# Attention and maxout feed-forward: weights cast to bf16 on their way in, by transfers that GpSimd queues

## The chip, the cores and the metric

The kernel runs on one core of a Trainium2 chip. A core has a matrix engine (TensorE, PE in the profile, with PEld for its weight loads), three engines for elementwise work (VectorE or DVE, ScalarE or ACT, GpSimd or POOL), and SyncE (SP), which here only queues transfers between the chip's memory and the core's on-chip memory. Sixteen DMA engines carry the transfers out. The metric is the device time of one execution in microseconds (us).

## The reference

The inputs are q, k and v of shape 4 x 8 x 768 x 64 (batch, heads, sequence, head size) and four weight matrices, all fp32. Attention is local, with a few global keys and a distance bias; its output feeds a maxout feed-forward:

```python
scores = scale * np.matmul(q, k.transpose(0, 1, 3, 2))
keep = (pos[None, :] < 8) | ((rel >= 0) & (rel < 96))   # rel = query position - key position
scores = np.where(keep, scores - slope[h] * dist, -1e9)
a = softmax(scores)
x = (a @ v) as (3072, 512)
h = np.maximum(np.maximum(x @ w1, x @ w2), x @ w3)      # w1, w2, w3: 512 x 768
out = h @ w_out                                         # w_out: 768 x 512
```

## The kernel before

The 3072 tokens are 24 tiles of 128, six for each batch. Attention of a tile needs only its own keys, those of the tile before it and the eight global keys, so it is a small job. The feed-forward works on chunks of 4, 2, 2, 4, 4, 4 and 4 tiles, and most of TensorE's work is there.

Everything is cut into units, and one long string, `SCHEDULE`, lists them in the order in which each engine, and each transfer queue, gets its instructions. Each engine then runs its own instructions strictly in this order and waits where an operand or a buffer is not ready. A unit is a letter with numbers. Where there is a last number that says who copies or casts, 0 is ScalarE, 1 VectorE and 2 GpSimd, 3 and 4 are mixtures or a transpose by DMA. The units that matter here:

- `l`, `v`, `L`: loads of q and k (512 KB each for the parts of the first twelve tiles, 256 KB for q or k of a later tile) and of v (256 KB a tile), queued by SP (lines 158, 174 and 167). `c` and `C` cast them to bf16 (lines 183, 189 and 198), `x` and `X` transpose q and k (tile `tpp`, line 239). `l0.0` and `l0.1` stand ahead of the string. Part 0 of the `l` and `x` units holds tiles 0 and 1, part 1 tiles 2 and 3, part 2 tiles 4 and 5, part 3 tiles 6 to 9. `l2.1` is k of tiles 4 and 5, `l3.0` a half of the heads of q of tiles 6 to 9.
- `G`, `V`: overwrite the first eight rows of a tile's k or v with the global ones (lines 214 to 216, and 221).
- `S`: scores of a tile for four heads, with the exponential on ScalarE. The mask and bias come either by a matmul against a bias tile ahead of the scores (last number 1, line 275) or by a multiplication on VectorE afterwards (unit `M`, line 307). `K` and `B` build the two kinds of tables.
- `A`: attention times v (lines 322 and 325), then the division by the row sum on VectorE (331 and 332). `T`: transpose of the result into `xT` (line 349).
- `F c.f.j`: chunk c, hidden block f (128 wide), weight matrix j: four matmuls (line 361) and a copy or maximum. `O`: the output product of a tile (line 376), its copy, and the store by SP (line 383). `E`: the last of these.
- `D`: matmuls on zeros at the start (line 436).
- `w g.j`, `o i`: loads of weights, queued by SP, fp32, into staging buffers (`wst`, `wost`, lines 417 and 422). `w0.j` is columns 0 to 255 of matrix j (512 KB), `w1.j` columns 256 to 767 (1 MB), `o` a third of w_out (512 KB).
- `W g.j`, `Q i`: casts of staged weights to bf16 into the tiles `w123` (three tiles, by column block) and `wo` (lines 427 and 430).

So a weight passes through an SP transfer, a staging buffer and a cast. The three `W` casts of columns 0 to 255 read `w0`, the other six read a half each of `w1`. There are three buffers of each size, and `o` shares those of `w0`.

Of the kernel before, what the change touches and what calls it, by code (L numbers as in the profile page):

```python
# [22 lines left out]


SCHEDULE = """
    K0 K1 K2 l1.0 B0.2 B1.1 B2.1 K3 K4 K5 K6 B3.0 B4.1 l1.1 D1.4 B5.0 c0.0.2 B6.0 c0.1.1 D0.4 v0 l2.0
    x0.0.3 K7 x0.1.4 c1.0.1 v1 l2.1 B7.0 S0.0.1 S0.1.1 G0.2 S1.0.0 M0.0 M0.1 c1.1.1 c2.0.2 x1.0.2 x1.1.0
    C0.1.1 A0.0 S1.1.1 G1.1 v2 v3 S2.0.1 S2.1.0 G2.1 T0.1 M1.0 M1.1 c2.1.1 S3.0.1 M2.0 M2.1 C1.1.2
    C2.1.1 M3.0 S3.1.1 M3.1 A1.0 V1.2 x2.0.2 C3.1.2 w0.0 A2.1 x2.1.0 V2.2 A3.0 T1.0 w0.1 G3.2 W0.0.2
    T2.1 T3.1 S4.0.0 S4.1.0 w0.2 F0.0.0 F0.1.0 W0.2.1 G4.2 w1.0 W0.1.2 F0.0.1 F0.1.1 F0.0.2 F0.1.2  # L30
    S5.0.0 S5.1.0 V3.2 M4.0 W1.0.2 F0.2.0 M4.1 M5.0 F0.3.0 v4 w1.1 W2.1.0 W2.0.2 F0.4.0 F0.5.0 W1.1.1
    C4.1.2 w1.2 W1.2.2 M5.1 v5 A4.1 l3.0 l3.2 l3.1 C5.1.0 V4.2 F0.2.1 c3.0.0 F0.3.1 F0.4.1 T4.0 F0.5.1
    A5.1 F0.2.2 c3.2.0 F0.3.2 W2.2.2 F0.4.2 x3.0.2 T5.1 F0.5.2 x3.2.1 F1.0.0 F1.1.0 l3.3 l4.0 F1.0.1
    F1.1.1 c3.1.2 c3.3.2 F1.0.2 x3.1.4 F1.2.0 F1.2.1 x3.3.1 F1.3.0 c4.0.0 o2 F1.1.2 o1 Q1.1 F1.4.0 Q2.2
    S6.0.0 S6.1.0 G6.2 M6.0 o0 F1.5.0 F1.2.2 F1.3.1 S7.0.0 S7.1.0 v6 l4.1 v7 F1.4.1 G7.0 M6.1 v8 F1.3.2
    x4.0.0 L12 v9 M7.0 L13 Q0.2 O0.0.1 S8.0.0 M7.1 c4.1.1 S8.1.0 C6.1.2 F1.5.1 O0.1.0 A6.0 x4.1.2 C7.1.2
    A7.1 V7.1 G8.2 F1.4.2 F1.5.2 S9.0.0 S9.1.0 G9.2 v10 T6.1 M8.0 O0.2.1 T7.1 C8.1.0 v11 S10.0.0 S10.1.0
    G10.0 M8.1 M9.0 M9.1 O0.3.0 A8.0 F2.0.0 V8.2 F2.1.0 F2.0.1 F2.1.1 C9.1.2 C12.0.2 C13.0.2 C10.1.0
    F2.0.2 F2.1.2 A9.1 M10.0 M10.1 V9.1 X12.0 F2.2.0 F2.3.0 S11.0.0 S11.1.0 T8.4 M11.0 X13.4 F2.4.0 L14
    O1.0.1 L15 T9.0 F2.2.1 A10.1 F2.5.0 V10.2 F2.3.1 F2.4.1 S12.0.0 S12.1.0 M11.1 M12.0 F2.2.2 F2.3.2  # L40
    F2.4.2 v12 C11.1.2 A11.0 C14.0.0 X14.4 T10.0 v13 v14 M12.1 v15 F2.5.1 C12.1.2 F2.5.2 O1.1.1 G12.1
    S13.0.0 S13.1.0 G13.1 T11.1 O2.0.0 F3.0.0 M13.0 F3.0.1 M13.1 F3.1.0 F3.2.0 A12.1 C15.0.0 F3.0.2
    S14.0.0 X15.4 S14.1.0 T12.4 C13.1.1 F3.1.1 F3.2.1 v16 L16 L17 G14.0 L18 A13.0 F3.1.2 F3.2.2 F3.3.0
    M14.0 T13.1 F3.3.1 F3.3.2 V13.2 S15.0.0 S15.1.0 G15.0 F3.4.0 C14.1.2 F3.5.0 M14.1 M15.0 M15.1 A14.0
    V14.2 F3.4.1 F3.5.1 T14.4 F3.4.2 C15.1.2 F3.5.2 A15.0 L19 v17 C16.0.2 C17.0.2 X16.0 O2.1.0 X17.4
    T15.1 S16.0.0 v18 v19 S16.1.0 C18.0.2 G16.0 M16.0 O3.0.1 O3.1.1 F4.0.0 V15.2 F4.1.0 F4.2.0 F4.3.0
    C16.1.2 M16.1 A16.1 C19.0.2 X18.3 X19.4 F4.0.1 F4.0.2 S17.0.0 S17.1.0 M17.0 F4.1.1 C17.1.1 F4.1.2
    S18.0.0 S18.1.0 C18.1.1 F4.2.1 F4.3.1 T16.4 M17.1 F4.2.2 F4.3.2 G18.0 S19.0.0 M18.0 M18.1 L20 M19.0
    C19.1.1 L21 S19.1.0 F4.4.0 F4.5.0 G19.2 V16.2 C20.0.0 L22 A17.0 F4.4.1 M19.1 F4.5.1 F4.4.2 F4.5.2
    X20.4 T17.4 A18.1 T18.4 A19.0 T19.4 O3.2.0 O3.3.0 C21.0.1 C22.0.0 O4.0.0 S20.0.0 S20.1.0 M20.0 X21.4  # L50
    v20 G20.0 V19.1 M20.1 O4.1.0 F5.0.0 F5.1.0 F5.2.0 F5.0.1 F5.1.1 S21.0.0 S21.1.0 F5.0.2 F5.3.0 F5.1.2
    C20.1.2 A20.1 G21.1 X22.4 V20.2 F5.4.0 L23 F5.5.0 S22.0.0 S22.1.0 v21 v22 v23 C21.1.2 C22.1.2
    C23.0.0 X23.4 M21.0 M21.1 M22.0 F5.2.1 F5.3.1 F5.4.1 F5.5.1 F5.2.2 C23.1.1 F5.3.2 A21.1 F5.4.2
    F5.5.2 G22.2 S23.0.0 T20.4 S23.1.0 T21.4 O4.2.0 M22.1 M23.0 M23.1 V21.2 A22.0 O4.3.0 V22.2 A23.1
    T22.4 T23.4 O5.0.0 O5.1.0 O5.2.0 O5.3.0 F6.0.0 F6.1.0 F6.2.0 F6.0.1 F6.1.1 F6.0.2 F6.2.1 F6.1.2
    F6.3.0 F6.2.2 F6.4.0 F6.5.0 F6.3.1 F6.4.1 F6.3.2 F6.4.2 F6.5.1 F6.5.2 E
"""


# [1 line left out]
def kernel(  # L61
# [293 lines left out]
    def u_F1(c, f, j):  # L355
        W = len(chunks[c]) * 128
        if f == 0 and j == 0:
            ht[c] = ht_pool.tile([128, NF, W], BF16, name="ht", tag="ht")
        ps = psH.tile([128, W], FP32, name="h", tag="h")
        for dm in range(4):  # L360
            nc.tensor.matmul(ps, w123[f // 2][:, dm, j, (f % 2) * 128:(f % 2) * 128 + 128],  # L361
                             xT[c][:, dm], start=(dm == 0), stop=(dm == 3))
# [49 lines left out]
    def load_w(g, j):

        n = 256 * (1 + g)
        st = stage_pool.tile([128, 4, n], FP32, name="wst", tag=f"wst{g}")
# [1 line left out]
        nc.sync.dma_start(out=st, in_=wsrc[j][:, 256 * g:256 * g + n].rearrange("(i p) f -> p i f", p=128))
# [92 lines left out]
```

## Time and profile before

| | |
|---|---|
| median of 17 runs | 181.29 us (180.58 to 183.16) |
| the profiled execution | 181.41 us, of which the span from first to last instruction is 179.6 us |
| HBM read, written | 25.17 MB, 6.29 MB |
| SP queue (q1) | 83424 packets, 35.20 MB |
| first F matmul starts | 23.85 us |
| `w0`, `w1` transfer, issue to landing | 7.0 us (512 KB), 10.7 us (1 MB), medians |
| casts of weights | POOL 1038 ns x6 and 1042 ns x2, DVE 787 ns x2 and 1565 ns x1, ACT 1078 ns x1 |

Times in the views are microseconds from the first instruction; "x" gives the number of instructions. A chain of waits is followed back from the last instruction to whatever released each step. Matmul ends are modelled and matmuls overlap, so PE's busy time says little about how full it is; the list of its waits says more. The DMA share is the mean busy share of sixteen engines and passes 1 where packets overlap.

### The profile page before, as it was taken

How to read it: one execution, taken by the hardware profiler on the slowest of the kernel's cores; microseconds unless marked ns; L12 is line 12 of the kernel's file. 1: busy time of each engine (PE TensorE's matmuls, PEld its weight loads, DVE VectorE, ACT ScalarE, POOL GpSimd, SP SyncE). 2: the span in 40 equal slices, each digit the busy share in tenths (PEclk: the TensorE clock that was granted, in tenths of full speed). 3: DMA queues.
4: the chain of work that ended last, by engine and by line, in shares of the span. 5: the costliest groups of instructions: out<-in, count | busy, mean ns of one | idle time of the engine just before them, and what ended most of it. 6: DMA issues, size and time to landing. Idle time of an engine off the chain costs nothing.

```text
span 179.6 us, 3985 instructions
## 1 busy us (share of the span) xinstructions
PE 169.5 (94%) x1556; PEld 95.7 (53%) x1556; DVE 121.6 (68%) x236; ACT 103.2 (57%) x158; POOL 38.8 (22%) x66
## 2 busy tenths in 40 slices
PE   7587799999999999999999999999999999999991
PEld 2343644558867687755555554454445555444450
DVE  4566548788998988957887648996346994053810
ACT  4999664853787956569162566344965353513031
POOL 6313555424430152010224600100011211000000
PEclk9999999999999999999999999999999999999999
DMA  5999999999999658997499999954999624700014
GB/s 138 290 263 250 337 341 385 318 335 367 258 215 252 157 148 204 202 205 153 99 223 180 237 181 269 227 103 95 210 234 218 118 50 146 262 0 4 0 67 167
DMA packets 83586, 35.51 MB, mean 198 GB/s; under 512 B 66160, under 2 KB 78320, under 8 KB 83568
## 3 DMA queue, kind: packets, MB, share of 16 engines
q1 hardware_dynamic: 83424, 35.20, 84.8%
q8 instruction: 12, 0.20, 0.5%
q10 hardware_dynamic: 144, 0.07, 0.1%
q14 instruction: 6, 0.05, 0.1%
HBM read 25.17 MB, written 6.29 MB: 175 GB/s over the span
## 4 chain that ended last, share of the span: by engine, by line
PE 84%; SPq 5%; DMA 4%; issue 3%; POOL 1%; DVE 1%; ACT 0%; ACTq 0%; POOLq 0%
PE h L361 53%; PE po L376 17%; PE sp L283 6%; SPq L158 3%; DMA rawp<-in_k_dram 3%; PE op L322 3%; PE op L325 3%; SPq L174 2%; PE tpp L239 1%; PE xtp L349 1%; DMA out_dram<-ost 1%; PE tp L261 1%; POOL va L221 0%; DVE xb L332 0%; POOL va L189 0%
## 5 line engine op out<-in xcount | busy, mean ns | idle before, releaser
L361 PE MATMUL h<-xT,w 128*128 128x512 bf16 (+1 forms) x504 | 100.1, 349 | 0.1
L361 PEld LDWEIGHTS <-w 128*128 128x128 bf16 x504 | 47.0, 98 | 40.7 <-issue 0.6
L288 ACT ACTIVATE P<-sp 128x1024 bf16<-128x1024 f32 (+1 forms) x48 | 43.3, 954 | 21.7 <-PE sp L283 21.3
L368 DVE TENSOR_TENSOR h<-h,h 128x512 bf16<-128x512 bf16 (+1 forms) x42 | 25.3, 608 | 19.0 <-PE h L361 18.5
L376 PE MATMUL po<-wo,ht 128*128 128x512 bf16 (+2 forms) x156 | 33.6, 363 | 0.0
L366 ACT CAST h<-h 128x512 bf16<-128x512 f32 (+1 forms) x42 | 21.6, 534 | 19.2 <-PE h L361 18.6
L307 DVE TENSOR_TENSOR P<-P,wmask 128x1024 bf16<-128x1024 bf16 x36 | 25.3, 716 | 7.4 <-ACT P L288 7.3
L370 DVE TENSOR_TENSOR ht<-h,h 128x512 bf16<-128x512 bf16 (+1 forms) x42 | 25.2, 607 | 5.2 <-PE h L361 4.2
L376 PEld LDWEIGHTS <-ht 128*128 128x128 bf16 x156 | 14.1, 98 | 13.8
L382 ACT COPY ost<-po 128x512 f32<-128x512 f32 (+2 forms) x19 | 10.6, 561 | 18.1 <-PE po L376 15.6
L332 DVE TENSOR_TENSOR xb<-op,rz 128x512 bf16<-128x512 f32 x24 | 16.6, 691 | 0.8
L283 PEld LDWEIGHTS <-qkT 64*128 64x128 bf16 x352 | 10.0, 94 | 9.1 <-issue 7.8
L283 PE MATMUL sp<-qkT 64*128 64x128 bf16 x352 | 14.7, 219 | 0.0
L322 PEld LDWEIGHTS <-P 128*128 128x128 bf16 x192 | 12.5, 97 | 3.5 <-DVE P L307 0.5
L221 POOL COPY va<-vaf 8x260 int32<-8x260 int32 x13 | 6.2, 478 | 35.6 <-PE op L325 32.3
L322 PE MATMUL op<-va,P 128*128 128x65 bf16 x160 | 12.6, 193 | 1.1 <-POOL va L189 0.8
L189 POOL CAST va<-rawv 128x512 bf16<-128x512 f32 x12 | 7.6, 633 | 23.1 <-PE h L361 17.4
L325 PEld LDWEIGHTS <-P 128*128 128x128 bf16 x160 | 10.5, 97 | 2.3 <-issue 0.9
L243 ACT COPY qkT<-tpp 128x1024 bf16<-128x1024 bf16 (+1 forms) x9 | 8.2, 920 | 3.5 <-PE tpp L239 3.2
L239 PE MATMUL tpp<-identb,qkp 128*128 128x128 bf16 x96 | 8.2, 234 | 2.0 <-POOL qkp L183 1.6
L325 PE MATMUL op<-va,P 128*128 128x65 bf16 x128 | 9.9, 193 | 0.2 <-POOL va L221 0.2
L331 DVE RECIPROCAL rz<-op 128x8 f32<-128x8 f32 x24 | 4.9, 204 | 7.4 <-PE op L325 5.7
(69 smaller groups left out, 114.2 us busy)
## 6 DMA issues: line engine op xcount, KB each, us to landing
rawv<-in_v_dram SPq DMA_DIRECT2D x24, 256.0 KB, 5.3
out_dram<-ost SPq DMA_DIRECT2D x23, 256.0 KB, 2.3
rawp<-in_q_dram SPq DMA_DIRECT2D x6, 512.0 KB, 7.3
rawp<-in_k_dram SPq DMA_DIRECT2D x6, 512.0 KB, 7.3
wst<-in_moe_w_dram SPq DMA_DIRECT2D x3, 1024.0 KB, 10.7
raw<-in_q_dram SPq DMA_DIRECT2D x12, 256.0 KB, 4.9
raw<-in_k_dram SPq DMA_DIRECT2D x12, 256.0 KB, 4.9
wst<-in_moe_w_dram SPq DMA_DIRECT2D x3, 512.0 KB, 7.0
```

The source lines that it names most:

```text
L283: nc.tensor.matmul(sp[:, hh, j2, ds], qT(T - ds, 1)[hsl, jp], qT(T, 0)[hsl, jp], start=not how, stop=True, skip_group_check=True)
L288: nc.scalar.activation(P[:, :, 0:n], sp.rearrange("p a b d n -> p (a b) d n")[:, :, 0:n], AF.Exp, bias=0.0, scale=scale)
L307: nc.vector.tensor_mul(P, P, wmask[:, g, :, 0:2])
L322: nc.tensor.matmul(o, P[:, i, 0], heads(va[T])[:, h], start=True, stop=(t == 0), skip_group_check=True)
L325: nc.tensor.matmul(o, P[:, i, 1], heads(va[T - 1])[:, h], start=False, stop=True, skip_group_check=True)
L332: nc.vector.tensor_tensor(out=x.rearrange("p (g h) d -> p g h d", g=2), in0=o4[:, :, :, 0:64], in1=rz[:, :, :, None].to_broadcast([128, 2, ...
L361: nc.tensor.matmul(ps, w123[f // 2][:, dm, j, (f % 2) * 128:(f % 2) * 128 + 128], xT[c][:, dm], start=(dm == 0), stop=(dm == 3))
L366: nc.scalar.copy(h01, ps)
L368: nc.vector.tensor_max(h01s[c, f], h01s[c, f], ps)
L370: nc.vector.tensor_max(ht[c][:, f], h01s[c, f], ps)
L376: nc.tensor.matmul(po, ht[c][:, f, tt * 128:(tt + 1) * 128], wo[:, f, cols], start=(f == 0), stop=(f == NF - 1))
L382: copy(ost, po)
```

## The change

SP no longer loads the weights. GpSimd queues them, in one transfer each from fp32 in memory to bf16 in the persistent tile, with the same rows and sizes at the source. The staging pool is gone. The units `W` and `Q` remain in the string but do nothing. `w123` is one tile in place of three; each F matmul waits for the transfer that brought its columns. `SCHEDULE` is a different string from its first line to its last: the order of units, and who copies or casts what, are new, while the units of loads, scores, attention and feed-forward are the same in number. The `D` units no longer occur. Scores with the bias by matmul are now S0.0, S0.1, S1.1, S2.1, S3.0, S3.1, S4.0 and S6.0; before they were S0.0, S0.1, S1.1, S2.0, S3.0 and S3.1.

In the new order SP's first transfers are: q and k of part 0, q and k of part 1, q of part 2, v of tiles 0, 1, 2, 3, k of part 2 (`l2.1`), `l3.0`, `l3.2`, v of tiles 4 and 5. GpSimd's instructions after its set-up are: two q casts, cast of v of tile 0, `w0.0`, cast of v of tile 1, `w0.1`, `w0.2`, `w1.0`, `w1.1`, patch V2.2, `w1.2`, cast of `l3.0`, cast of `l3.1`, the three `o`. VectorE casts `l2.1` ahead of v of tile 3.

The start of the string, up to the first F units:

```diff
-    K0 K1 K2 l1.0 B0.2 B1.1 B2.1 K3 K4 K5 K6 B3.0 B4.1 l1.1 D1.4 B5.0 c0.0.2 B6.0 c0.1.1 D0.4 v0 l2.0
-    x0.0.3 K7 x0.1.4 c1.0.1 v1 l2.1 B7.0 S0.0.1 S0.1.1 G0.2 S1.0.0 M0.0 M0.1 c1.1.1 c2.0.2 x1.0.2 x1.1.0
-    C0.1.1 A0.0 S1.1.1 G1.1 v2 v3 S2.0.1 S2.1.0 G2.1 T0.1 M1.0 M1.1 c2.1.1 S3.0.1 M2.0 M2.1 C1.1.2
-    C2.1.1 M3.0 S3.1.1 M3.1 A1.0 V1.2 x2.0.2 C3.1.2 w0.0 A2.1 x2.1.0 V2.2 A3.0 T1.0 w0.1 G3.2 W0.0.2
-    T2.1 T3.1 S4.0.0 S4.1.0 w0.2 F0.0.0 F0.1.0 W0.2.1 G4.2 w1.0 W0.1.2 F0.0.1 F0.1.1 F0.0.2 F0.1.2
...
+    K0 l1.0 l1.1 K1 l2.0 c0.0.0 B0.2 B1.1 B2.1 B3.1 B4.0 B5.2 K2 x0.0.3 c0.1.0 x0.1.4 K3 K4 S0.0.1 K5
+    B6.1 c1.0.2 v0 x1.0.0 B7.1 S0.1.1 G0.0 c1.1.1 v1 c2.0.2 S1.0.0 x1.1.4 S1.1.1 G1.1 x2.0.3 C0.1.2
+    S2.0.0 w0.0 C1.1.2 v2 S2.1.1 w0.1 K6 M0.0 K7 M0.1 w0.2 M1.0 M1.1 w1.0 A0.0 v3 G2.0 w1.1 M2.0 A1.1
+    V1.1 W0.2.1 C2.1.0 S3.0.1 l2.1 c2.1.1 S3.1.1 C3.1.1 M2.1 A2.0 G3.1 x2.1.2 T0.0 V2.2 w1.2 M3.0 M3.1
+    A3.1 T1.0 S4.0.1 l3.0 l3.2 v4 v5 W0.0.0 W1.0.1 T2.1 T3.1 S4.1.0 c3.0.2 c3.2.1 l3.1 c3.1.2 V3.1
+    W0.1.2 W2.1.1 l3.3 W1.1.1 G4.1 x3.0.2 F0.0.0 F0.1.0 M4.0 M4.1 l4.0 v6 W2.2.2 S5.0.0 S5.1.0 v7 o1
+    x3.2.3 l4.1 F0.0.1 F0.1.1 W1.2.1 o2 o0 S6.0.1 W2.0.1 F0.0.2 F0.1.2 Q0.1 M5.0 M5.1 C4.1.0 A4.1 F0.2.0
...
```

The functions:

```diff
-    stage_pool = ctx.enter_context(tc.tile_pool(name="stage", bufs=3))
...
-    w123 = [persist.tile([128, 4, 3, 256], BF16, name=f"w123_{i}") for i in range(3)]
+    w123 = persist.tile([128, 4, 3, DFF], BF16, name="w123")
...
-            nc.tensor.matmul(ps, w123[f // 2][:, dm, j, (f % 2) * 128:(f % 2) * 128 + 128],
+            nc.tensor.matmul(ps, w123[:, dm, j, f * 128:f * 128 + 128],
                              xT[c][:, dm], start=(dm == 0), stop=(dm == 3))
...
         n = 256 * (1 + g)
-        st = stage_pool.tile([128, 4, n], FP32, name="wst", tag=f"wst{g}")
-        wst[g, j] = st
-        nc.sync.dma_start(out=st, in_=wsrc[j][:, 256 * g:256 * g + n].rearrange("(i p) f -> p i f", p=128))
+        nc.gpsimd.dma_start(out=w123[:, :, j, 256 * g:256 * g + n],
+                            in_=wsrc[j][:, 256 * g:256 * g + n].rearrange("(i p) f -> p i f", p=128))
...
     def load_wo(i):
-        st = stage_pool.tile([128, 2, DM], FP32, name="wost", tag="wst0")
-        wst["o", i] = st
-        nc.sync.dma_start(out=st, in_=moe_w_out[i * 256:(i + 1) * 256, :].rearrange(
-            "(i p) f -> p i f", p=128))
+        nc.gpsimd.dma_start(out=wo[:, 2 * i:2 * i + 2],
+                            in_=moe_w_out[i * 256:(i + 1) * 256, :].rearrange("(i p) f -> p i f", p=128))
...
     def cast_w(g, j, how):
-        src = wst[0, j] if g == 0 else wst[1, j][:, :, 256 * (g - 1):256 * g]
-        copies[how](w123[g][:, :, j], src)
+        pass
...
     def cast_wo(i, how):
-        copies[how](wo[:, 2 * i:2 * i + 2], wst["o", i])
+        pass
```

More of the change, by code (lines that the diff above doesn't have):

```diff
@@ L31 @@
[L31 to L55, printed above, removed]
@@ L56 @@
-    F6.3.0 F6.2.2 F6.4.0 F6.5.0 F6.3.1 F6.4.1 F6.3.2 F6.4.2 F6.5.1 F6.5.2 E
+    K0 l1.0 l1.1 K1 l2.0 c0.0.0 B0.2 B1.1 B2.1 B3.1 B4.0 B5.2 K2 x0.0.3 c0.1.0 x0.1.4 K3 K4 S0.0.1 K5
[3 more added lines that the diff above has]
+    A3.1 T1.0 S4.0.1 l3.0 l3.2 v4 v5 W0.0.0 W1.0.1 T2.1 T3.1 S4.1.0 c3.0.2 c3.2.1 l3.1 c3.1.2 V3.1
@@ new lines @@
+    W0.1.2 W2.1.1 l3.3 W1.1.1 G4.1 x3.0.2 F0.0.0 F0.1.0 M4.0 M4.1 l4.0 v6 W2.2.2 S5.0.0 S5.1.0 v7 o1
+    x3.2.3 l4.1 F0.0.1 F0.1.1 W1.2.1 o2 o0 S6.0.1 W2.0.1 F0.0.2 F0.1.2 Q0.1 M5.0 M5.1 C4.1.0 A4.1 F0.2.0
+    F0.3.0 F0.4.0 F0.5.0 V4.1 C5.1.1 T4.1 A5.0 M6.0 F0.2.1 F0.3.1 F0.4.1 F0.5.1 F0.2.2 F0.3.2 F0.4.2
+    T5.0 x3.1.2 c3.3.1 F0.5.2 x3.3.0 v8 v9 F1.0.0 F1.0.1 F1.0.2 S6.1.0 G6.2 M6.1 S7.0.0 F1.1.0 F1.2.0
+    S7.1.0 F1.1.1 c4.0.2 x4.0.4 C6.1.2 F1.3.0 F1.4.0 C7.1.0 G7.2 M7.0 M7.1 S8.0.0 S8.1.0 F1.2.1 F1.3.1
@@ new lines @@
+    F1.4.1 F1.1.2 F1.2.2 Q2.2 F1.3.2 F1.4.2 G8.2 L12 c4.1.0 C12.0.2 A6.1 F1.5.0 A7.0 x4.1.0 C8.1.0 Q1.0
+    O0.0.0 M8.0 M8.1 T6.1 v10 S9.0.0 V7.1 M9.0 S9.1.0 M9.1 v11 v12 O0.1.0 O0.2.1 A8.0 T7.0 O0.3.0 F2.0.0
+    V8.2 G9.2 S10.0.0 S10.1.0 G10.2 F1.5.1 L13 F2.0.1 L14 T8.0 C9.1.1 C10.1.2 C11.1.0 F1.5.2 F2.0.2
+    M10.0 S11.0.0 M10.1 M11.0 S11.1.0 M11.1 C13.0.2 F2.1.0 X12.1 O1.0.0 A9.1 F2.2.0 F2.3.0 O1.1.1 F2.1.1
+    T9.0 V9.2 A10.0 V10.2 F2.2.1 F2.3.1 F2.4.0 S12.0.0 S12.1.0 X13.4 F2.1.2 F2.5.0 T10.0 L15 A11.0
@@ new lines @@
+    F2.4.1 F2.5.1 F2.2.2 C14.0.2 X14.4 T11.0 G12.1 S13.0.0 S13.1.0 v13 F2.3.2 F2.4.2 F2.5.2 F3.0.0
+    F3.1.0 M12.0 M12.1 F3.0.1 G13.1 F3.0.2 L16 M13.0 v14 L17 M13.1 F3.2.0 S14.0.0 S14.1.0 M14.0 F3.1.1
+    F3.2.1 C12.1.2 A12.0 C13.1.0 L18 C14.1.0 C15.0.2 X15.1 M14.1 F3.3.0 v15 F3.4.0 F3.3.1 A13.0 V13.2
+    T12.4 F3.1.2 C16.0.0 A14.1 G14.1 C17.0.1 F3.5.0 X16.4 X17.4 F3.2.2 F3.4.1 C18.0.1 T13.4 S15.0.0
+    S15.1.0 M15.0 T14.4 F3.5.1 F3.3.2 M15.1 F3.4.2 V14.2 X18.0 L19 L20 v16 v17 O2.0.0 C15.1.2 A15.1
@@ new lines @@
+    O2.1.1 T15.1 F3.5.2 G15.0 S16.0.0 S16.1.0 G16.1 F4.0.0 F4.1.0 S17.0.0 S17.1.0 M16.0 F4.2.0 F4.0.1
+    F4.1.1 S18.0.0 S18.1.0 V15.1 F4.0.2 C19.0.2 M16.1 M17.0 C16.1.2 X19.4 O3.0.0 v18 M17.1 C17.1.0 M18.0
+    C18.1.2 F4.3.0 A16.1 O3.1.1 V16.1 F4.1.2 T16.4 v19 C19.1.2 O3.2.1 G18.0 v20 S19.0.0 S19.1.0 M18.1
+    M19.0 M19.1 O3.3.0 C20.0.0 X20.4 F4.4.0 F4.2.1 A17.1 F4.5.0 T17.4 F4.2.2 A18.1 T18.4 F4.3.1 A19.0
+    F4.4.1 F4.5.1 V19.2 F4.3.2 F4.4.2 G19.0 S20.0.0 S20.1.0 M20.0 T19.4 F4.5.2 L21 C20.1.2 L22 C21.0.3
@@ new lines @@
+    F5.0.0 F5.1.0 G20.1 M20.1 F5.0.1 F5.1.1 F5.0.2 F5.1.2 A20.1 F5.2.0 X21.4 L23 C22.0.3 X22.4 F5.3.0
+    F5.4.0 F5.2.1 F5.3.1 C23.0.1 v21 S21.0.0 M21.0 S21.1.0 G21.2 F5.5.0 V20.1 F5.4.1 v22 M21.1 S22.0.0
+    S22.1.0 G22.0 C21.1.2 C22.1.2 T20.4 F5.2.2 F5.3.2 X23.4 A21.0 M22.0 v23 C23.1.2 F5.5.1 F5.4.2 F5.5.2
+    S23.0.0 S23.1.0 O4.0.0 M22.1 M23.0 M23.1 O4.1.0 T21.4 V21.2 A22.0 V22.2 O4.2.0 T22.4 A23.1 T23.4
+    O4.3.0 O5.0.1 O5.1.0 O5.2.1 F6.0.0 F6.0.1 F6.1.0 F6.0.2 F6.1.1 F6.2.0 F6.3.0 F6.4.0 O5.3.1 F6.2.1
@@ L57 @@
+    F6.3.1 F6.4.1 F6.1.2 F6.5.0 F6.2.2 F6.3.2 F6.4.2 F6.5.1 F6.5.2 E
 """
```

## The prediction

> **What bounds the kernel now.** I read the page's header and chain of waits first, then a table of stages, then PE's waits stage by stage, then the timelines of SP and GpSimd up to 36 us. Header and chain:
>
> ```profile
> span 179.6 us, 3985 instructions
> PE 169.5 (94%) x1556; PEld 95.7 (53%) x1556; DVE 121.6 (68%) x236; ACT 103.2 (57%) x158; POOL 38.8 (22%) x66
> ...
> PE 84%; SPq 5%; DMA 4%; issue 3%; POOL 1%; DVE 1%; ACT 0%; ACTq 0%; POOLq 0%
> ```
>
> The chain is TensorE work except for a stretch of SP and DMA. The table of stages says where that lies (columns: window in us, its length, busy time of PE, PE's weight loads, DVE, ACT, POOL, then granted clock, DMA share, GB/s):
>
> ```profile
> 0.00:10.00 10.00, 7.02 (x36) 3.17 (x37) 5.69 (x20) 7.60 (x16) 5.13 (x15) 1.00 0.90 221
> 10.00:15.50 5.50, 4.46 (x68) 2.64 (x65) 2.71 (x7) 5.20 (x7) 1.69 (x3) 1.00 1.25 260
> 15.50:23.85 8.35, 6.21 (x113) 4.39 (x113) 5.88 (x13) 5.82 (x8) 2.57 (x6) 1.00 1.16 315
> 23.85:173.95 150.10, 150.06 (x1325) 84.14 (x1326) 107.08 (x196) 83.33 (x127) 29.37 (x44) 1.00 0.83 188
> ```
>
> From 23.85 us to 173.95 us PE is busy for 150.06 of 150.10 us. A busy PE is not proof of a full one, but the list of waits agrees: no PE wait of this stretch exceeds 0.4 us. 23.85 us is the start of the first matmul of the feed-forward (F0.0.0, line 361). So the end is that start plus a fixed length. Casts of the weights lie beside this wall of PE work or just ahead of it. What sets the 23.85 us is in the ordered chain (start, length, what):
>
> ```profile
> 10.24 5.10 DMA rawp<-in_k_dram
> 15.34 3.25 issue
> 18.59 0.40 POOL va L221
> ...
> 20.20 0.61 POOL va L189
> 20.81 0.35 POOL va L221
> ...
> 23.85 2.32 PE h L361 x10
> ```
>
> Loads, then the V of tile 3 (landed at 20.2), its cast and patch on GpSimd, A3, T3, S4, F0.0.0. DMA is saturated all this time (share above 1 from 5 us on). SP's queue is one line of transfers, and the weights stand after V of tile 3:
>
> ```profile
> 10.24 1.16 SPq L158 DMA_DIRECT2D rawp<-in_k_dram  x1
> 11.45 3.17 SPq L174 DMA_DIRECT2D rawv<-in_v_dram  x2
> 14.67 4.53 SPq L417 DMA_DIRECT2D wst<-in_moe_w_dram  x4
> 19.24 0.92 SPq L174 DMA_DIRECT2D rawv<-in_v_dram  x1
> 20.21 4.38 SPq L417 DMA_DIRECT2D wst<-in_moe_w_dram  x2
> ```
>
> The reader should keep two facts: only what comes before F0.0.0 counts, and there DMA bandwidth and its order are scarce.
>
> **What the Trainium skill says.** "DMA: Bandwidth & Descriptors", section SWDGE vs HWDGE vs iDMA: a transfer that casts must come from GpSimd, whose cores write the descriptors by software. No transfer of the kernel before takes this way, so no run here shows its price. The same page, section Queues, rings and completion order: each DMA engine alternates between the queues that have work, packet by packet. Before, all loads are in the one SP queue, so this is not seen either. The same page, section Latency and other measured facts, gives about 1 us to the first byte on the GpSimd path; I use it as my estimate of how long one such issue holds GpSimd. "SBUF — State Buffer", section Who interferes with whom: VectorE copies and casts in a two-port mode shut GpSimd out while they run, descriptor writing included. The trace has VectorE 70% busy (5.88 of 8.35 us) in the window 15.5 to 23.85, but of that only two fp32 casts, 0.69 and 0.42 us, are surely of this kind.
>
> **The change part by part.**
>
> Removed casts. Twelve casts go: six of w on POOL (1.04 us each), two on DVE (0.79), one on ACT (1.08), two of w_out on POOL (1.04), one on DVE (1.57). That is 8.3 us of POOL, 3.1 of DVE, 1.1 of ACT, and only the first (21.70 us, POOL) was before F0.0.0; it was done at 22.7, before F0.0.0. All others lie under the PE wall. Worth 0. Staging buffers: SP's weight issues waited for them about 1.3 us in all; worth 0 likewise.
>
> Removed from SP: nine issues, w and w_out. Their time on SP (14.67 to 19.2, 20.2 to 24.6) is mostly queue back-pressure and not work. What follows them, the loads of tiles 6 to 9, comes earlier in SP's order.
>
> The schedule string is new throughout. Counted unit by unit, PE's work is the same except: the eight warm-up matmuls are gone (1.17 to 4.76 us, in idle time), and S4.0 and S6.0 now take their bias by matmul, two more each. Four heads' bias costs 0.52 us (two of 128x512 at 15.67 to 16.19) for S4.0 and about 0.26 for S6.0. S4.0 is ahead of F0.0.0, S6.0 behind it. Also moved ahead of F0.0.0 is x3.0, eight transposes, 0.45 us by the chain. So from F0.0.0 to the end: 179.6 - 23.85 = 155.75, minus 0.45 plus 0.26 = 155.56. The profiled execution took 181.41 us, 1.81 beyond its span. **Time after = start of F0.0.0 + 157.4 us**, plus any hole in PE. (The profiled 181.41 is 0.12 above the median of 181.29: I ignore that.) The patches, copies and casts that moved between ACT, DVE and POOL cost nothing while PE stays full; the cover is the 150 us wall, where the least idle of the three others, DVE, has 43 us free.
>
> F0.0.0 in the new order. PE must have passed A3, T3, S4 and x3.0. These need: k of tiles 4, 5 (SP's 10th transfer; DVE casts it ahead of V of tile 3, so A3 waits for it too), and q of tiles 6 to 9 (SP's 11th; cast on POOL behind six weight issues). SP's first eleven transfers are seven of 0.5 MB and four of 0.25 MB: 4.5 MB. Before, F0.0.0 needed SP's first ten, 4.0 MB, and w0.0.
>
> When can they land? The traffic adds up, from the five-us windows (153, 289, 257, 278, 366, 346, 332 GB/s), to 0.77, 2.21, 3.50, 4.89, 6.72, 8.45, 10.1 MB at 5, 10, ... 35 us. A transfer lands when about 0.4 MB more than its place in the queue has moved (V of tile 0: place 2.25 MB, landed at 11.6 us, 2.65 MB moved). GpSimd casts V of tile 0 (place 2.75, so 3.15 MB, 13.7 us) and then issues w0.0 at 14.3; after casting V of tile 1 (3.4 MB, 14.6 us) it issues w0.1, w0.2, w1.0, w1.1 from 15.3 us on. From 15.5 us (3.63 MB moved) SP still has to move 4.9 - 3.5 = 1.4 MB for F0.0.0, and up to 4.5 MB of weights stand in another queue beside it. All depends on the share that SP keeps:
> - all of it (lower end): 4.9 MB at 20.1 us. Then the k of tiles 4, 5 is later by its tail: 4.4 MB at 18.3, plus two casts 1.1, A3 0.5, reciprocal and product 0.9, transposes 0.4, copy 0.43 and about 1 of queueing = 22.6 us.
> - half: 3.63 + 2.8 = 6.4 MB, 24.1 us; cast 1.04 and transposes 0.62: F0.0.0 at 25.8.
> - 40%: 3.63 + 3.5 = 7.1 MB, 26.1 us: F0.0.0 at 27.8 (the way over k of tiles 4, 5, 5.9 MB at 22.8 plus the same 4.3 us, gives 27.1 and is not last).
> - weights first (upper end): 3.63 + 1.4 + 4.5 = 9.5 MB, 33.1 us: F0.0.0 at 34.8.
>
> I take 40%. Row lengths (from the code: q and k of tiles 4, 5 512 B, V 256 B, weights 1 or 2 KB) pull towards the weights if engines alternate by rows; larger packets of rows pull towards half; and GpSimd may not fill its queue without gaps.
>
> Cost on GpSimd: with d us per weight issue, the patch V2.2 comes at 15.3 + 4d and the cast of q at about 15.7 + 5d. With d = 1 both are done by 21, hidden behind the landing at 26.1. The cover ends at d = (26.1 - 15.7)/5 = 2.1 us; beyond it each us costs five. What waits behind them is V2.2 (for A3), the cast of q, and through them all of PE. Bounds for d: 0.5 to 3 us.
>
> Sum: 27.8 + 157.4 = 185.2, nothing added for holes later: by the end of chunk 0, some 18 us on, only 6.5 MB of SP and the weights, 11 MB, are needed, and those had moved by 39 us before.
>
> **The rivals.**
> - Weights first: 34.8 + 157.4 = 192.2. For it: weight rows two to eight times longer. Against it: GpSimd has to write the rows fast enough.
> - GpSimd held: d = 3 gives the cast of q at 30.7, F0.0.0 at 32.4, 189.8. For it: four weight issues ahead of V2.2, VectorE busy beside. Against: nothing seen in this trace.
> - The other side, faster: SP keeps its bandwidth, because GpSimd's transfers start late or thinly. F0.0.0 at 22.6, 180.0. It decides from a share of about two thirds: q landing at 22.4 (5.75 MB) means 1.4 of 2.1 MB, F0.0.0 at 24.05, no change. For it: V of tile 3 has 0.5 MB less ahead of it on SP and no cast of w stands before F0.0.0. Against: the traffic before F0.0.0 is already saturated, and the new order needs 0.5 MB more.
> - Holes: the new order leaves gaps in the PE wall (ring buffers, transposes by DMA) of 1 to 4 us with F0.0.0 near 24: about 183.
>
> **How the numbers follow.** Forecast (share 30 to 60%, 182 to 188.5) 0.42; weights first 0.25; GpSimd held 0.08; holes 0.06; no change, by balance at two thirds, 0.05; faster 0.14. A change of 0.3% (0.5 us) is about what can be told apart. So faster 0.14, same 0.05, slower 0.81. The range runs from 181.0 to 192.5: it leaves out the faster case and the far end of GpSimd held.
>
> **What would show it.** In the profile after: the start of the first F matmul (27.8; 22.6 or 34.8 for the rivals); how long POOL is held per weight issue; when V of tile 3 and q of tiles 6 to 9 land; PE again without a hole from there to about 174 + 4. If PE has large gaps after F0.0.0, or F0.0.0 starts below 24, my sum is wrong; if F0.0.0 is late but waits for a weight transfer and not for q or V, the step on shares is wrong.

## The result, and the profile after

The kernel after takes 184.49 us (median of 8 runs, 184.18 to 184.74) against 181.39 us (47 runs of the kernel before, with those of the experiments): 1.0174 times as long, interval 1.0154 to 1.0194. The profiled execution took 184.38 us, 1.78 us more than its span. The page of the kernel after:

```profile
span 182.6 us, 3968 instructions
PE 167.0 (91%) x1552; PEld 95.2 (52%) x1552; DVE 121.6 (67%) x239; ACT 99.5 (54%) x155; POOL 36.7 (20%) x63
...
q1 hardware_dynamic: 79440, 28.91, 73.2%
q0 software_dynamic: 3984, 3.15, 11.1%
...
PE 75%; DMA 16%; SPq 4%; POOL 1%; ACT 1%; issue 0%; DVE 0%; ACTq 0%
...
w<-in_moe_w_dram POOLq DMA_DIRECT2D x3, 512.0 KB, 16.3
w<-in_moe_w_dram POOLq DMA_DIRECT2D x3, 256.0 KB, 9.2
```

There is a second queue now, q0. Its bytes, and the KB of the last two lines, are counted at the bf16 destination: 6.3 MB of fp32 are read for the 3.15 MB. The chain of waits has four times as much DMA in it (16% against 4%). The table of stages (columns as in the prediction):

```profile
15.50:24.97 9.47, 7.21 (x135) 5.00 (x130) 7.02 (x16) 8.51 (x13) 5.20 (x8) 1.00 1.26 256
24.97:177.00 152.03, 150.21 (x1320) 83.67 (x1318) 106.22 (x198) 77.47 (x120) 22.68 (x37) 1.00 0.82 167
```

PE's wall is no longer without gaps: 1.8 us of the 152.03 us in the second line are missing from its busy time. PE's timeline shows where. In the brackets stands the idle time ahead of a line, and who ended it:

```profile
24.40 0.62 PE L238 MATMUL tpp<-identb,qkp 128*128 128x128 bf16 x8 [1.20 <-POOL qkp L182]
24.86 1.89 PE L360 MATMUL h<-xT,w 128*128 128x512 bf16 x8
...
27.20 0.51 PE L282 MATMUL sp<-qkT 64*128 64x128 bf16 x12 [0.23 <-DVE qkT L215]
...
32.88 0.19 PE L321 MATMUL op<-va,P 128*128 128x65 bf16 x1 [0.62 <-ACT va L188]
...
38.16 0.20 PE L321 MATMUL op<-va,P 128*128 128x65 bf16 x1 [0.96 <-DVE va L188]
```

F0.0.0 starts at 24.86 us, right behind the transposes x3.0, which waited for the cast of `l3.0`. Then PE waits three times inside chunk 0, mostly for v of tiles 4 and 5. The ordered chain names what was behind the last of these:

```profile
14.10 0.90 POOL w L414
15.00 0.65 POOL va L188
15.64 0.49 SPq L157
16.14 0.05 issue
16.19 0.70 SPq L173
16.89 0.05 issue
16.94 20.72 DMA rawv<-in_v_dram
...
37.68 0.44 DVE va L188
38.12 0.05 issue
38.16 0.20 PE op L321
```

One transfer of 256 KB, v of tile 5, took 20.72 us. So the 2.97 us between the two profiled executions (184.38 - 181.41) are:

| part | us |
|---|---|
| F0.0.0 later, 24.86 against 23.85 | 1.01 |
| PE work moved: x3.0 ahead of F0.0.0, S6.0's bias behind it | -0.19 |
| waits inside chunk 0: 0.23, 0.62, 0.96 | 1.81 |
| rest, not itemised | 0.34 |

Transfers land at their issue plus the time "to landing" in the trace. The landings that the argument needs, for four of the runs below (us):

| | after | p2_w1late | p4_shortrows | q3_nocast |
|---|---|---|---|---|
| `w0.0`, `w0.1`, `w0.2` | 19.8, 24.7, 27.3 | 21.7, 24.7, 27.5 | | 20.2, 24.4, 26.2 |
| q `l3.0`, k `l3.2` (rows of 1 KB) | 23.3, 26.1 | 23.6, 26.6 | 22.9, 25.7 | 25.8, 32.6 |
| v of tiles 4, 5 (rows of 256 B) | 32.2, 37.6 | 28.4, 29.4 | 29.9, 34.1 | 37.4, 38.3 |
| `w1.0`, `w1.1`, `w1.2` | 30.7, 34.1, 37.4 | 32.2, 36.4, 40.5 | 31.3, 36.3, 42.0 | 29.7, 33.1, 36.6 |

How the two queues shared the DMA engines can be counted (queue, packets, MB at the destination, share of 16 engines). From 26.15 us, when `l3.2` had landed, to 32.18 us, when v of tile 4 landed, SP had only v of tiles 4 and 5 under way, a packet for each row of 256 B, and GpSimd almost only `w1`, a packet for each row of 2 KB (1 KB at the bf16 destination):

```profile
q0 software_dynamic: 934, 0.93, 90.9%
q1 hardware_dynamic: 935, 0.24, 29.9%
```

That is one packet of the one queue for one packet of the other, and so some 8 to 1 in bytes read. Before that, while `l3.0` was under way, GpSimd's first packet moved at 17.57 us, 3.5 us after the issue of `w0.0` began (14.04). From there to 23.26 us, when `l3.0` landed, the two queues moved about as many packets as each other, unevenly at first and from 21 us on one for one (381 and 382). `l3.0` and `w0` both have rows of 1 KB, so `l3.0` got about as many bytes as the weights beside it:

```profile
q0 software_dynamic: 1056, 0.53, 67.8%
q1 hardware_dynamic: 1067, 0.97, 58.3%
```

### The profile page after: what moved, and what is told of

It reads as the page before. It is cut to its first block, busy times and chain, and to the rows that moved or that the text cites. A ratio compares the mean times of both kernels' runs of the same rounds, so it can differ in the third digit from the quotient of the medians.

```text
span 182.6 us, 3968 instructions
## 1 busy us (share of the span) xinstructions
PE 167.0 (91%) x1552; PEld 95.2 (52%) x1552; DVE 121.6 (67%) x239; ACT 99.5 (54%) x155; POOL 36.7 (20%) x63
## 3 DMA queue, kind: packets, MB, share of 16 engines
q0 software_dynamic: 3984, 3.15, 11.1%
HBM read 25.17 MB, written 6.29 MB: 172 GB/s over the span
## 4 chain that ended last, share of the span: by engine, by line
PE 75%; DMA 16%; SPq 4%; POOL 1%; ACT 1%; issue 0%; DVE 0%; ACTq 0%
PE h L360 47%; PE po L375 16%; DMA rawv<-in_v_dram 15%; PE sp L282 5%; SPq L157 3%; PE op L321 3%; PE op L324 2%; DMA out_dram<-ost 1%; PE tpp L238 1%; PE xtp L348 1%; PE tp L260 1%; ACT ost L381 1%; POOL w L414 0%; SPq L173 0%; POOL va L188 0%
## 5 line engine op out<-in xcount | busy, mean ns | idle before, releaser
L287 ACT ACTIVATE P<-sp 128x1024 bf16<-128x1024 f32 (+1 forms) x48 | 43.9, 962 | 20.2 <-PE sp L282 19.9
L365 ACT CAST h<-h 128x512 bf16<-128x512 f32 (+1 forms) x42 | 21.9, 532 | 26.4 <-PE h L360 26.2
L306 DVE TENSOR_TENSOR P<-P,wmask 128x1024 bf16<-128x1024 bf16 x35 | 23.7, 695 | 3.4 <-ACT P L287 3.3
L381 ACT COPY ost<-po 128x512 f32<-128x512 f32 (+2 forms) x17 | 9.4, 557 | 14.9 <-PE po L375 13.8
L282 PE MATMUL sp<-qkT 64*128 64x128 bf16 x352 | 15.2, 219 | 0.2 <-DVE qkT L215 0.2
L381 DVE COPY ost<-po 128x512 f32<-128x512 f32 (+1 forms) x9 | 5.8, 646 | 13.4 <-PE po L375 9.0
L238 PEld LDWEIGHTS <-qkp 128*128 128x128 bf16 x96 | 6.6, 108 | 9.9 <-ACT qkp L182 7.1
L349 ACT COPY xT<-xtp 128x512 bf16<-128x512 bf16 x8 | 4.6, 590 | 11.5 <-PE xtp L348 11.5
L197 POOL CAST qkb<-raw 128x1024 bf16<-128x1024 f32 x5 | 5.5, 1091 | 21.0 <-DMA raw<-in_k_dram 21.0
```

The lines of the kernel that those rows point to most:

```text
L238: nc.tensor.transpose(tp[:, e, j - lo], qb["p", n, s][:, e, 2 * j:2 * j + 2].rearrange("i h d -> i (h d)"), identb)
L282: nc.tensor.matmul(sp[:, hh, j2, ds], qT(T - ds, 1)[hsl, jp], qT(T, 0)[hsl, jp], start=not how, stop=True, skip_group_check=True)
L287: nc.scalar.activation(P[:, :, 0:n], sp.rearrange("p a b d n -> p (a b) d n")[:, :, 0:n], AF.Exp, bias=0.0, scale=scale)
L306: nc.vector.tensor_mul(P, P, wmask[:, g, :, 0:2])
L381: copy(ost, po)
```

## The experiments

The theory: beside a weight transfer SP keeps a share of the bytes that goes with the length of its rows against the weights', so the loss is one of place and row length. The rivals: the new path costs by itself (GpSimd is held, or the cast burdens the DMA engines); or the new order of units loses time whatever the path. All ratios below are to the kernel before, with their 95% interval; short diffs are against the kernel after unless another is named.

**Path and order apart: p1_path and p3_order.** p1 has the functions of after with the string of before; p3 the functions of before with the string of after. The first line of each string shows which is which (minus: before and p1; plus: after and p3):

```diff
-    K0 l1.0 l1.1 K1 l2.0 c0.0.0 B0.2 B1.1 B2.1 B3.1 B4.0 B5.2 K2 x0.0.3 c0.1.0 x0.1.4 K3 K4 S0.0.1 K5
+    K0 K1 K2 l1.0 B0.2 B1.1 B2.1 K3 K4 K5 K6 B3.0 B4.1 l1.1 D1.4 B5.0 c0.0.2 B6.0 c0.1.1 D0.4 v0 l2.0
```

> The order of the kernel before, with only the way of the weights changed (GpSimd queue, cast on the way, W and Q empty). The weights then stand on GpSimd behind the cast of v of tile 3. Theory A (only the sharing of DMA bandwidth before chunk 0 costs anything; casts and staging are worth nothing): v of tile 3 lands earlier than 20.2 us, since no weights run beside it, w0.0 is issued only after it and is what F0.0.0 waits for; first F matmul at 23.5 to 26 us, total 181 to 183.5 us. Theory B (the new way is itself slow, GpSimd held or cast slow in the DMA engines): 184.5 us or more, with GpSimd instructions late behind the issues.

> The new order with the old way of the weights (SP queue, fp32 staging, casts where W and Q stand). In one queue all 4.5 MB of w stand ahead of q of tiles 6 to 9. Theory A (a first-come line of 9.0 MB, at the rate of the kernel before): that q lands at about 32 to 33 us, first F matmul at about 34, total near 191. Rival D (the order alone makes the 3 us and the way of the weights is free): 184.5, first F matmul near 25.

p1: 190.67 us, 1.0461 (1.0402 to 1.0519). GpSimd's timeline, then PE's:

```profile
20.18 0.61 POOL L188 CAST va<-rawv 128x512 bf16<-128x512 f32 x1 [1.29 <-DMA rawv<-in_v_dram]
20.73 0.95 POOL L414 DMA_DIRECT2D w<-in_moe_w_dram  x1
```

```profile
29.67 0.61 PE L360 MATMUL h<-xT,w 128*128 128x512 bf16 x1 [4.67 <-DMA w<-in_moe_w_dram]
...
38.97 3.63 PE L360 MATMUL h<-xT,w 128*128 128x512 bf16 x15 [1.01 <-DMA w<-in_moe_w_dram]
```

In the old string `w0.0` stands behind the cast of v of tile 3. On SP that cost nothing, as SP does not cast; on GpSimd the issue itself waits for that v to land. It came at 20.73 us, and beside SP's full queue it took until 29.6. PE waited 4.67 us for it and 1.01 us for a later one.

p3: 207.44 us, 1.1381 (1.1318 to 1.1443), some 16 us above the 191 that its theory gave. VectorE:

```profile
30.17 0.69 DVE L183 CAST qkp<-rawp 128x1024 bf16<-128x1024 f32 x1 [9.02 <-DMA rawp<-in_k_dram]
```

In one queue the new place of the weights puts them ahead of `l2.1`, k of tiles 4 and 5, which landed at 30.15 us in place of 18.8. F0.0.0 started at 37.14; later PE waited another 5.57 us and 2.40 us behind casts of w_out, and each of these two waits came with a stretch at half the clock (last section). The casts stood where the string of after has its empty `W` and `Q` units, so how much of p3's loss is the places of the casts isn't told apart. Neither half of the change works alone: each path needs its own place for the weights.

**Row length and place: p4_shortrows and p2_w1late.** p4 splits each `w1` transfer in two, with 1 KB rows in place of 2 KB, same bytes and same place. p2 keeps the rows and moves the three `w1` behind the cast `c3.0.2`, which waits for `l3.0`.

```diff
-        nc.gpsimd.dma_start(out=w123[:, :, j, 256 * g:256 * g + n],
-                            in_=wsrc[j][:, 256 * g:256 * g + n].rearrange("(i p) f -> p i f", p=128))
+        for lo in range(256 * g, 256 * g + n, 256):
+            hi = lo + 256
+            nc.gpsimd.dma_start(out=w123[:, :, j, lo:hi],
+                                in_=wsrc[j][:, lo:hi].rearrange("(i p) f -> p i f", p=128))
```

```diff
+    S4.0.1 l3.0 l3.2 v4 v5 W0.0.0 W1.0.1 T2.1 T3.1 S4.1.0 c3.0.2 w1.0 w1.1 w1.2 c3.2.1 l3.1 c3.1.2 V3.1
```

> The changed kernel with each 1 MB weight transfer split in two of 256 columns, so that every weight row is 1 KB instead of 2 KB; bytes and place unchanged, three more issues on GpSimd (about 0.75 us each, hidden before V2.2). Theory E (DMA engines alternate between the two queues row by row, so SP's share follows the ratio of row lengths): SP's share beside w1 doubles, v of tile 5 lands at 31 to 34 us instead of 37.7, the waits for v in chunk 0 shrink below 0.5 us in all, total 183 to 184. Rival F (they alternate by bytes or larger packets): v of tile 5 within 1.5 us of 37.7, total 184.2 to 185.

> The changed kernel with its three 1 MB weight transfers (w1.0, w1.1, w1.2) moved on GpSimd behind the cast of q of tiles 6 to 9. Theory A (weights with long rows crowd out SP's loads): v of tile 5 lands before 32 us instead of 37.7, first F matmul near 23 instead of 24.9, both waits for v inside chunk 0 (0.6 and 1.0 us) vanish; w1.0 lands by about 30 us, before F0.2.0 needs it; total 180.3 to 182. Rival C (the bytes are the limit, their order is not): F0.2.0 waits for w1.0, the holes move there, total 184 or more.

The loads of v of tiles 4 and 5, from the view of that tile in the window 15 to 18 us, in after, p4 and p2:

```profile
DMA to landing us min/median/max: 16.0/18.4/20.7
```

```profile
DMA to landing us min/median/max: 13.7/15.5/17.2
```

```profile
DMA to landing us min/median/max: 12.3/12.4/12.5
```

p4: 182.89 us, 1.0077 (1.0054 to 1.01). v of tile 5 landed at 34.1 in place of 37.6 us, and PE's two waits for v are gone; a wait of 0.43 us for the last weights is new. The count from the landing of `l3.2` (25.67 us) to that of v of tile 4 (29.91 us) is one for one here too, now with 1 KB read for each packet of GpSimd, so 4 to 1 in bytes, which is the ratio of the rows:

```profile
q0 software_dynamic: 1023, 0.51, 86.9%
q1 hardware_dynamic: 1024, 0.26, 46.2%
```

p2: 182.93 us, 1.0072 (1.0051 to 1.0094). The waits for v are gone here too, but F0.0.0 came at 25.20 us, not earlier, since `l3.0` landed at 23.6: `w1` had not been what held `l3.0`. No run took `w0` away from beside `l3.0`; that `w0` and the 0.5 MB more ahead of F0.0.0 make it late is read from the trace of after and not shown by a run.

Both take half of the loss away with nothing changed in path or cast. The cause of the waits in chunk 0 is shown.

**The start of F0.0.0: q1_x3later, q2_x3later_w1late, r1_fix.** q1 is p4 with x3.0 behind the first two F; q2 is q1 with `w1` moved as in p2; r1 is q1 with the cast of `l3.2` moved behind M4.1 and its transposes behind F0.1.1. q1 against p4:

```diff
-    W0.1.2 W2.1.1 l3.3 W1.1.1 G4.1 x3.0.2 F0.0.0 F0.1.0 M4.0 M4.1 l4.0 v6 W2.2.2 S5.0.0 S5.1.0 v7 o1
+    W0.1.2 W2.1.1 l3.3 W1.1.1 G4.1 F0.0.0 F0.1.0 x3.0.2 M4.0 M4.1 l4.0 v6 W2.2.2 S5.0.0 S5.1.0 v7 o1 x3.2.3
```

> The changed kernel with the 1 MB weight transfers split into rows of 1 KB (as in p4) and, in addition, the transposes x3.0 moved from ahead of F0.0.0 to behind F0.1.0. Theory A2 (x3.0's wait for q of tiles 6 to 9 is all that holds the first F matmul; the weight w0.0 and chunk 0's input are there): first F matmul at 23.4 to 23.7 us instead of 24.5, total 181.5 to 182.3. Rival (something else, w0.0 or the scores, holds it too): no earlier than 24.2, total as p4, 182.6 to 183.2.

> As q1, and the rows of 1 MB weights also issued only after the cast of q of tiles 6 to 9. Theory A2: v of tiles 4 and 5 land before 30 us, first F matmul at 23.4 to 23.7, no wait inside chunk 0 for v; w1.0 lands at about 31 to 32 and F0.2.0 waits under 0.5 us for it: total 181.0 to 182.0, within 0.3% of the kernel before. Rival C: the weights, now late and in short rows, miss F0.2.0 or the second matrix's turn by 1 us or more, total 182.5 to 184.

> As q1, and two units moved out of the way: the cast of k of tiles 6 to 9 (c3.2, which held VectorE until 26.5 us and with it the global keys of tile 4 and S5) behind M4.1, and the transposes x3.2 behind F0.1.1. Theory: q1's gain of 0.8 us at F0.0.0 was eaten by a 1.3 us wait of S5 behind this cast; without it PE has no wait over 0.5 us after F0.0.0 at about 23.7, total 181.0 to 181.9. Rival: the landing of the weights or of v takes the place of the wait, total 182.5 or more.

F0.0.0 started at 23.75, 23.91 and 23.50 us, as early as before. The times were 182.97 us (1.0077, 1.0046 to 1.0108), 183.98 us (1.0131, 1.0095 to 1.0167) and 182.92 us (1.0081, 1.0052 to 1.011): nothing gained on p4. PE's timelines of q1 and r1:

```profile
27.57 0.51 PE L278 MATMUL sp<-qkT 64*128 64x128 bf16 x12 [1.26 <-DVE qkT L211]
```

```profile
30.21 0.29 PE L278 MATMUL sp<-qkT 64*128 64x128 bf16 x4 [1.32 <-DVE qkT L238]
```

In q1 the scores of tile 5 wait for a key patch on VectorE that stands behind the cast of `l3.2`, whose load lands at 26.5 us. Moving that cast (r1) brings the wait to the scores of tile 6, which need the transposes of the same load. What x3.0 had cost was only the first in a row of waits for loads that the new order needs early: `l3.2` landed at 38.2 us in the kernel before, and PE did not wait for it there. q2 had the same wait (1.16 us) and two more for weights (0.62 and 0.29 us), which now came too late.

**The cast itself: q3_nocast and q4_casttwice.** q3 keeps GpSimd's queue and place, but moves fp32 into staging tiles and casts on the engines, at new places in the string. q4 is the kernel before with each weight cast done twice.

```diff
+        st = stage_pool.tile([128, 4, n], FP32, name="wst", tag=f"wst{g}")
+        wst[g, j] = st
+        nc.gpsimd.dma_start(out=st, in_=wsrc[j][:, 256 * g:256 * g + n].rearrange("(i p) f -> p i f", p=128))
...
+        src = wst[0, j] if g == 0 else wst[1, j][:, :, 256 * (g - 1):256 * g]
+        copies[how](w123[:, :, j, 256 * g:256 * g + 256], src)
```

```diff
-        copies[how](w123[g][:, :, j], src)
+        for _ in range(2):
+            copies[how](w123[g][:, :, j], src)
```

> The changed kernel with the weights still queued by GpSimd at the same places, but moved as fp32 into staging buffers and cast by the engines just ahead of their use (the casts are placed anew in the order; the three w_out transfers come after chunk 0). It separates the second queue from the cast inside the transfer. Theory Q (the second queue with its long rows is what hurts; the cast in the transfer costs the DMA engines nothing much): q of tiles 6 to 9 within 1 us of 23.3, v of tile 5 within 2 us of 37.7, total 184 to 187. Rival K (the cast makes the transfers slow): v of tile 5 lands 4 us or more earlier and the waits for v vanish.

> The kernel before with each of its twelve weight casts done twice (8.3 us more on GpSimd, 3.1 on VectorE, 1.1 on ScalarE). Prediction's step (casts lie under full PE work and are worth nothing): total within 0.5 us of 181.4. Rival (they are partly on the path, so removing them was worth something): slower by 1 us or more.

q3: 196.31 us, 1.0787 (1.0726 to 1.0848), much slower than expected. The weights landed when they did in after (36.6 against 37.4 us for the last), so the cast in the transfer is not seen to delay them. But SP's loads came later than in after. The queue line of q3's page says why, and beside it p4's:

```profile
q0 software_dynamic: 1680, 6.29, 9.0%
```

```profile
q0 software_dynamic: 5568, 3.15, 12.1%
```

Each transfer ends with one further packet of 4 B on each of 16 engines: the trace lists 144 of them for nine transfers and 192 for p4's twelve. Without them after has 3840 packets, which is its number of rows (1536 of `w0`, 1536 of `w1`, 768 of w_out); p4 has 5376, again its rows. q3 has 1536 for 6.29 MB, 4 KB each. "DMA: Bandwidth & Descriptors", section Queues, rings and completion order, in the Trainium skill says that an engine drains one whole packet of a queue before it turns to the next queue. The counts agree: one for one in after and p4 (above), and in q3 from 21 us to the landing of `l3.2` (32.55 us) 917 packets of 4 KB against 915 of SP's, now 3.50 against 0.75 MB. Only the first microseconds of GpSimd's queue don't fit: in q3 from 17.63 to 21 us it got 192 packets to SP's 522, and why is open. The same section calls 9 to 17 descriptors typical of a packet; the trace doesn't show descriptors, only that what it lists as a packet is one row in the casting transfers. So without the cast GpSimd's packets are larger, and SP keeps less.

In q3's PE timeline stand a wait of 3.18 us ahead of x3.0 for `l3.0`, and waits for casts of weights:

```profile
26.91 0.62 PE L235 MATMUL tpp<-identb,qkp 128*128 128x128 bf16 x8 [3.18 <-POOL qkp L179]
29.58 3.60 PE L357 MATMUL h<-xT,w 128*128 128x512 bf16 x8 [2.05 <-ACT w L423]
...
38.28 1.90 PE L357 MATMUL h<-xT,w 128*128 128x512 bf16 x8 [1.02 <-DVE w L423]
...
42.50 3.63 PE L357 MATMUL h<-xT,w 128*128 128x512 bf16 x16 [1.84 <-POOL w L423]
```

The eight matmuls of the second line take 3.60 us; the same eight take 1.89 us in after. That is the matrix engine's clock, which was at half here; more at the end. How much of q3's loss is the places that I chose for the casts isn't told apart.

q4: 185.49 us, 1.0222 (1.0189 to 1.0255), where no change was expected. PE's timeline, from F0.0.0 on (which stays at 23.85):

```profile
26.46 3.63 PE L361 MATMUL h<-xT,w 128*128 128x512 bf16 x16 [0.71 <-POOL w L428]
...
35.93 2.77 PE L361 MATMUL h<-xT,w 128*128 128x512 bf16 x12 [1.24 <-ACT h L366]
...
54.46 0.60 PE L361 MATMUL h<-xT,w 128*128 128x256 bf16 x4 [1.48 <-DVE ht L370]
```

The casts of before lie under PE's work, but with little slack behind them: a second cast of about 1 us shows up as a wait on each of the three engines. Doubling gives no price for removing; r3 below does.

**The new path at places by need: q5_hoist, r2_hoistall, r3_hoistwo.** All three have the functions of after and the string of before, with the weights moved ahead of the loads that GpSimd's casts wait for. q5 has `w0` behind C1.1.2 and `w1` in 1 KB rows at its old place; r2 has 2 KB rows and `w1.0` behind V1.2, the other two behind G3.2; r3 is r2 with `o0` right behind `o1`. The first of the diffs is r2 and r3 against the string of before, the second r3 against r2:

```diff
-    C2.1.1 M3.0 S3.1.1 M3.1 A1.0 V1.2 x2.0.2 C3.1.2 w0.0 A2.1 x2.1.0 V2.2 A3.0 T1.0 w0.1 G3.2 W0.0.2
+    M2.1 C1.1.2 w0.0 w0.1 w0.2 C2.1.1 M3.0 S3.1.1 M3.1 A1.0 V1.2 w1.0 x2.0.2 C3.1.2 A2.1 x2.1.0 V2.2 A3.0
+    T1.0 G3.2 w1.1 w1.2 W0.0.2 T2.1 T3.1 S4.0.0 S4.1.0 F0.0.0 F0.1.0 W0.2.1 G4.2 W0.1.2 F0.0.1 F0.1.1 F0.0.2 F0.1.2
```

```diff
-    F1.3.0 c4.0.0 o2 F1.1.2 o1 Q1.1 F1.4.0 Q2.2 S6.0.0 S6.1.0 G6.2 M6.0 o0 F1.5.0 F1.2.2 F1.3.1 S7.0.0 S7.1.0
+    F1.3.0 c4.0.0 o2 F1.1.2 o1 o0 Q1.1 F1.4.0 Q2.2 S6.0.0 S6.1.0 G6.2 M6.0 F1.5.0 F1.2.2 F1.3.1 S7.0.0 S7.1.0
```

> The order of the kernel before with the new way of the weights, as p1, but w0.0, w0.1 and w0.2 placed on GpSimd behind the cast of v of tile 1 (about 15 us) instead of behind that of v of tile 3 (20.7 us), and the 1 MB ones in rows of 1 KB. Theory P (p1 lost its time to the late place of w0 and the 8.9 us that w0.0 took beside SP's loads): w0.0 lands by 22 to 24, first F matmul at 24 to 25.5, total 181.6 to 184. Theory B (the new way is slow in itself): first F matmul still after 27, total 185 or more.

> The order of the kernel before with the new way of the weights, all six w transfers placed early on GpSimd: w0.0, w0.1, w0.2 behind the cast of v of tile 1, w1.0 behind the patch V1.2, w1.1 and w1.2 behind the key patch of tile 3; rows of 2 KB. SP's loads that are behind are not needed for 10 us and more in this order. Theory P (the new way costs nothing when its place fits the need; the casts it saves were worth nothing): first F matmul at 23.6 to 24.2, no wait for a weight over 0.5 us, total 181.0 to 182.0, the same as before within 0.4%. Theory B (the new way costs in itself): 183 or more. If the saved casts are worth something after all: below 180.8.

> As r2, with the third w_out transfer issued right behind the other two (41.5 to 43.6 us) instead of behind a key copy that holds GpSimd until 48.3. Theory P (the new way, placed by need, costs nothing, and the casts it saves were worth nothing): the 1.1 us wait of the first output product for w_out goes, no other takes its place, total 181.2 to 182.2, within 0.5% of the kernel before. Rival (another wait takes its place, or the new way costs by itself): 182.8 or more. If the saved casts count after all: below 180.8.

q5: F0.0.0 at 23.70 us, as expected, but 187.91 us, 1.035 (1.0298 to 1.0402). PE's timeline:

```profile
32.88 6.41 PE L356 MATMUL h<-xT,w 128*128 128x512 bf16 x16 [3.29 <-DMA w<-in_moe_w_dram]
```

The first half of `w1.0` was issued only at 24.1 us and landed at 32.8. r2: 183.53 us, 1.014 (1.0085 to 1.0194); no weight is late any more but w_out, for which the first O waited 1.07 us. r3: 182.08 us (22 runs), 1.0032 (1.0012 to 1.0051). Its one PE wait behind F0.0.0 (23.88 us) is:

```profile
30.21 3.63 PE L356 MATMUL h<-xT,w 128*128 128x512 bf16 x16 [0.44 <-DMA w<-in_moe_w_dram]
```

So the path by itself costs next to nothing where each weight is issued in time, and the twelve casts saved gain nothing: the kernel before had no wait in its wall that they could have taken away, and F0.0.0 came no earlier (23.88 against 23.85 us). r3 is the best version with the new path; it does not beat the kernel before.

## Why the prediction was right or wrong

The total, 185.2 us, is 0.7 us above what was measured, but its two terms were off by 2.9 and 2.1 us in opposite directions; that the total came so close is luck.

- **The form of the sum held.** F0.0.0 at 24.86 plus 157.4 gives 182.3. Of the 2.1 us that are missing up to 184.4, 1.8 are PE's waits behind F0.0.0, which the text had as the open term.
- **The share of SP was mis-sized.** "I take 40%" put F0.0.0 at 27.8 us. From 15.5 us until `l3.0` landed at 23.26, SP moved 1.51 MB (the prediction had 1.4, with 512 KB counted as 0.5 MB) and GpSimd read 1.06 MB of weights: a share of 59%, the upper end of the forecast's 30 to 60%. Two things made it larger than 40%. SP had the engines to itself until 17.57 us: GpSimd's first packet came 3.5 us after its issue began, where the prediction quotes about 1 us to the first byte. And the row lengths were named as what decides, but not those of `l3.0`, the transfer that ends the stretch: they are 1 KB, as long as those of `w0`, so that from 17.57 us on SP kept 48% of the bytes. With 59% the prediction's own sum gives 1.4 / 0.59 = 2.4 MB from 15.5 us on, a landing at 23.0 and F0.0.0 at 24.7. The term, F0.0.0 later than before, was 1.0 us in place of 3.95.
- **"Nothing added for holes later" failed.** It compared the sum of bytes needed by the end of chunk 0 with the sum moved. The sum was there, but not the right bytes: v of tiles 4 and 5, with 256 B rows, stood beside `w1`'s 2 KB rows and crept, while `w1.2` landed at 37.4 us where 40.5 was still in time (p2, with no wait for it). The cost was 1.8 us. The rival of holes, 1 to 4 us with F0.0.0 near 24, given 0.06, is closer to what happened than the forecast.
- **GpSimd held: rightly ranked low.** The estimate was 1 us an issue, hidden up to 2.1. The trace of after:

```profile
15.55 2.98 POOL L414 DMA_DIRECT2D w<-in_moe_w_dram  x4
20.28 0.39 POOL L220 COPY va<-vaf 8x260 int32<-8x260 int32 x1 [1.75 <-PE op L324]
20.73 0.74 POOL L414 DMA_DIRECT2D w<-in_moe_w_dram  x1
23.31 1.03 POOL L182 CAST qkp<-rawp 128x1024 bf16<-128x1024 f32 x1 [1.83 <-DMA rawp<-in_q_dram]
```

  Four issues take 2.98 us, 0.75 each. The patch V2.2 behind them still waits for PE, and the cast of `l3.0` for its load. The lock-out by VectorE, which the prediction cited from "SBUF — State Buffer", section Who interferes with whom, isn't seen here: the six issues last 0.745 to 0.954 us.
- **Weights first and faster: both wrong for `l3.0`.** Weights first describes what befell v of tiles 4 and 5, though.
- **Casts and staging worth 0: right as to the gain** (r3). But the cover named, 43 us free on the least idle engine over the whole wall, was no measure of it: q4 shows that at single places a cast of about 1 us more is not covered.
- **Not tried by itself**: the eight warm-up matmuls taken away, and the casts and patches that changed engine.

## What to carry to other kernels

A load that gets a queue of its own does not get bandwidth of its own: ask which transfers stand beside it while it runs and how large the packets of each queue are, since a small-row load beside a large-row one can crawl at an eighth of the other's pace. Compare what has landed transfer by transfer against when it is needed, not sums of bytes. A transfer moved to an engine that also computes starts only when the work ahead of it there is done, so its place has to be chosen anew, and a gain at one wait is worth only the distance to the next one.
